# A retention, convolution and expert kernel on one core: the quarter tiles' pieces placed one or two hooks later, and their expert index read once

## The chip, the cores and the metric

The kernel runs on one core of one Trainium2 chip. The metric is the device time of an execution in microseconds (us). Times shown as "before" are the median of three executions and the range of the three; the profile is of one more execution, taken by the hardware profiler.

## The reference

Three layers follow one another. Only the last one is touched by the change:

```python
def _moe2_ref(x, w_gate, w_local, w1, w2):
    B, S, D = x.shape                      # 2, 768, 512; 8 experts, F = 1024
    logits = einsum('bsd,de->bse', x, w_gate)
    local_gate = sigmoid(x @ w_local)
    for b in range(B):
        prev_e = -1
        for s in range(S):
            fresh_e = argmax(logits[b, s])
            e = fresh_e if s == 0 or local_gate[b, s] < 0.5 else prev_e
            prev_e = e
            p = softmax(logits[b, s])
            h = maximum(x[b, s] @ w1[e], 0.0)
            out[b, s] = p[e] * (h @ w2[e])
```

Here x is the output of a retention layer (state and outer products over 768 steps, 8 heads) followed by a gated feed-forward layer with a convolution of three taps. Every token goes to exactly one expert, which is found only at run time.

## The kernel before, in words

The first 230 us compute the retention layer, the feed-forward layer and the routing. What the change touches is the expert stage, the function `experts` (line 958), which runs for the rest of the time.

The tokens are sorted by expert into **tiles** of 128 tokens (eleven are handled by this stage, j = 0 to 10) and into **quarters** of 32 tokens for what an expert has left over. Four quarters, each with an expert of its own, make one **group**; there are two, g = 0 and 1. A tile's matmuls run in three passes over weights split into a high and a low part (`mm3`, lines 134 to 136). A group's matmuls run once, in plain 32-bit floats, and need the weights of four experts.

*Weights of a tile.* `fetch(j, which)` (line 699) issues four transfers of 512 KB from SP's queue, for the first matrix (which = 0) or the second. From tile 1 on it first reads the expert's index from the table `ei` into a register (`expert_at`, line 691), and from tile 2 on also a flag that says whether this tile's expert differs from that of tile j - 2, whose weights sit in the same buffer. If it doesn't, the four transfers are issued and move nothing. `cut(j, which, i)` (line 725) splits half of a fetched matrix on ACT and DVE, and `g1`, `g2` multiply with the halves.

*Weights of a group.* `fetch_q(g, which, i)` (line 713) fetches the i-th quarter of the first or second matrix of four experts: four transfers of 512 KB (line 723), each preceded by a read of that expert's index (line 692). We call such four transfers a **piece**: a0 to a3 are the pieces of group 0's first matrices, b0 to b3 those of its second, and A0 to A3, B0 to B3 those of group 1. Two buffers take turns for the pieces: `qc` (even ones) and `qs1l` (odd ones). A new piece can be fetched only when the matmuls of the piece two before it are done, which is why `fetch_q` of the next pieces is called from within the group's own code (`follow`). Pieces a0 and a1 are fetched ahead.

*The order of the work.* Every engine runs its instructions in the order in which the code writes them. The tiles' code calls `hook()` (line 951) after each half of `g1` and of `g2`: twice ahead of the loop, then four times per tile, so that hook 4j+3 follows the first half of g1 of tile j+1, 4j+4 its second half, 4j+5 the first half of g2 of tile j and 4j+6 its second half. The groups are generators (`group`, line 894) with seven steps: 1 turn the 32 x 4 token rows (line 818), 2 the matmuls with the first two pieces (line 916), 3 those with the next two, 4 the relu, 5 turn the hidden rows, 6 and 7 the matmuls with the b pieces, two each (line 938). The list `QT` (line 947) names the hooks at which the next step is written. A step that calls `follow` writes the next `fetch_q` at that place of SP's queue too.

```python
QT = [3, 8, 8, 9, 13, 18] + [19, 22, 26, 26, 27, 31, 36]
```

Step 1 of group 0 isn't in the list: it stands in the loop's code, right after the first half of g1 of tile 1.

Of the kernel before, what the change touches and what calls it, by code (L numbers as in the profile page):

```python
# [29 lines left out]
NTILE = 16  # L30
# [62 lines left out]
def tile_kernel(ctx, tc, cat, cst, qT, kT, kN, vN, w_in, conv_w, w_out, wg, w1, w2, out):  # L93
# [346 lines left out]
    for i in range(len(seq) + LOOK):  # L440
        if i < len(seq):
            p, c = seq[i]
# [12 lines left out]
        if i >= LOOK:  # L455
            p, c = seq[i - LOOK]
# [226 lines left out]
    SLOT = ["s0h", "s0l", "s1h", "c5"]  # L683
    QSLOT = ["c4", "s1l"]
    ncut, nq = [0], [0]
    W, QW = {}, {}

    def home(tag):
        return big if tag[0] == "s" else ws if tag == "c4" else wx

    def expert_at(n):
        return sy.value_load(ei[0:1, 0, n:n + 1], min_val=0, max_val=E - 1)  # L692
# [6 lines left out]
    def fetch(j, which, parts=range(4)):  # L699

        src = (w1, w2)[which].rearrange("e p a n -> e p (a n)")
        kw = {}
        if j == 0:
            src = src[0]
        else:
            src = src[bass.ds(expert_at(j), 1)].rearrange("o p n -> (o p) n")
            if j > 1:
                kw = dict(cond=sy.value_load(ei[0:1, 1, j:j + 1], min_val=0, max_val=1), cond_hint=True)
        dst = raw(j % 2, which)
        for i in parts:  # L710
            sy.dma_start(out=dst[:, i, :], in_=src[:, i * 1024:(i + 1) * 1024], **kw)

    def fetch_q(g, which, i, parts=range(4)):

        if (g, which, i) not in QW:
            tag = QSLOT[nq[0] % 2]
            nq[0] += 1
            QW[g, which, i] = home(tag).tile([P, 4, 1024], F32, tag=tag, name="q" + tag)
        w = QW[g, which, i]
        src = (w1, w2)[which].rearrange("e p a n -> e p (a n)")  # L720
        for u in parts:
            one_e = src[bass.ds(expert_at(NTILE + 4 * g + u), 1)].rearrange("o p n -> (o p) n")
            sy.dma_start(out=w[:, u, :], in_=one_e[:, i * 1024:(i + 1) * 1024])  # L723

    def cut(j, which, i):

        tag = SLOT[ncut[0] % len(SLOT)]
        ncut[0] += 1
        w = home(tag).tile([P, 2, 2, 1024], F32R, tag=tag, name="w" + tag)
        for h in range(2):  # L730
            r = RAW[j % 2, which][:, 2 * i + h, :]
            se.activation(out=w[:, 0, h, :], in_=r, func=AF.Copy)  # L732
            ve.tensor_tensor(out=w[:, 1, h, :], in0=r, in1=w[:, 0, h, :].bitcast(F32), op=ALU.subtract)  # L733
        W[j, which, i] = w.rearrange("p s h n -> p s (h n)")
# [3 lines left out]
    def gather(j, n=NT):  # L738

        X[j] = xg = xpool[0].tile([P, DM], F32, name="xg")  # L740
        po.memset(xg, 0.0)
        return po.indirect_dma_start(out=xg, out_offset=None, in_=xs[0:n], in_offset=bass.IndirectOffsetOnAxis(ap=it[:, j:j + 1], axis=0),  # L742
                                     bounds_check=n - 1, oob_is_err=False)
# [45 lines left out]
    for n, (t, m) in enumerate(units, 1):  # L789
        ffn_out(1, t, (m,))  # L790
        for step in STEPS.get(n, ()):
            next(step, done)
        if n in (20, 28):
            cut(0, 0, n // 28)
        if n == 27:
            for j in range(2):
                gather(j, NT - 2 * P)
        if n == 32:
            fetch(1, 0)
        if n == 40:  # L800
            fetch_q(0, 0, 0)
# [26 lines left out]
    def begin_x(j):  # L828

        x, X[j] = X[j], psb.tile([P, 4, P], F32, tag="b", name="tp")  # L830
        for k in range(4):
            te.matmul(X[j][:, k, :], x[:, k * P:(k + 1) * P], ident, start=(k == 0), stop=False, skip_group_check=True)
        late_x(j, 0)
# [6 lines left out]
    def turn_x(j):  # L840

        if j < 2:
            late_x(j, 1)
        hi, lo = (wk.tile([P, 4, P], F32R, name="x" + n) for n in "hl")
        x = X.pop(j)
        ps = x if j < 2 else turn(x, 0)
        split(ps, hi, lo)
        XT[j] = hi, lo

    def turn_h(j):  # L850

        t = [wk.tile([P, 8, P], F32R, name="t" + n) for n in "hl"]
        hr = HR.pop(j)
        ps = [turn(hr, i) for i in (0, 4)]
        for i in (0, 4):
            split(ps[i // 4], t[0][:, i:i + 4, :], t[1][:, i:i + 4, :])
        return t

    def g1(j, i, h):
        xh, xl = XT[j]  # L860
        w = W.pop((j, 0, i))
        for n in range(2):
            for k in (2 * i, 2 * i + 1):
                o = slice((k % 2) * F + n * 512, (k % 2) * F + (n + 1) * 512)
                mm3(h[n], xh[:, k, :], xl[:, k, :], w[:, 0, o], w[:, 1, o], k == 0, k == 3)

    def relu(j, h):
        HR[j] = hr = wk.tile([P, F], F32, name="hr")
        for n in range(2):
            se.activation(out=hr[:, n * 512:(n + 1) * 512], in_=h[n], func=AF.Relu)  # L870

    def g2(j, i, t, y):
        hh, hl = t
        w = W.pop((j, 1, i))
        for k in range(4 * i, 4 * i + 4):
            o = slice((k % 4) * DM, (k % 4 + 1) * DM)
            mm3(y, hh[:, k, :], hl[:, k, :], w[:, 0, o], w[:, 1, o], k == 0, k == 7)

    def finish(j, last=False):
        if last:  # L880
            yo = wk.tile([P, F], F32, tag="hr", name="yo")[:, 0:DM]
        elif j >= NTILE:
            yo = wk.tile([P, F], F32, tag="hq", name="yo", bufs=1)[:, 0:DM]
        else:
            yo = wk.tile([P, DM], F32, name="yo", bufs=1)
        se.activation(out=yo, in_=Y.pop(j), func=AF.Copy, scale=pr[:, j:j + 1])  # L886
        po.indirect_dma_start(out=rows_of[j], out_offset=bass.IndirectOffsetOnAxis(ap=it[:, j:j + 1], axis=0),  # L887
                              in_=yo, in_offset=None, bounds_check=NT - 1, oob_is_err=False)

    def tile_g1():  # L890
        return [psa.tile([P, 512], F32, tag=f"a{n}", name="g1") for n in range(2)]


    def group(g, ahead=None):
# [6 lines left out]
        def follow():  # L901
            p = pieces.pop(0)
            if p and p not in QW:
                fetch_q(*p)
# [39 lines left out]
                yield  # L944


    QT = [3, 8, 8, 9, 13, 18] + [19, 22, 26, 26, 27, 31, 36]
    groups = []
    hooks = [0]

    def hook():
        hooks[0] += 1
        while QT and QT[0] <= hooks[0]:
            QT.pop(0)
            while groups and next(groups[0], done) is done:
                groups.pop(0)

    def experts(n):

        fetch_q(0, 0, 1)  # L960
        fetch(1, 1)
        for j in range(2):
            begin_x(j)
        for j in range(2):
            turn_x(j)
        gather(NTILE)
        gather(2)
        groups.extend(group(g, g + 1 < QSTAT) for g in range(QSTAT))
        h = tile_g1()
        for i in range(2):  # L970
            g1(0, i, h)
            cut(1, 0, i)
            if i:
                relu(0, h)
            hook()
        cut(0, 1, 0)
        fetch(2, 0)
        T = {}
        for j in range(n):
            last, ahead = j + 1 == n, j + 2 < n  # L980
            if j + 3 < n:
                fetch(j + 3, 0)
            if j > 0:
                finish(j - 1)
            if j + 3 < n:
                gather(j + 3)
            if j == 2:
                gather(NTILE + 1)
            if j not in T and j > 0:
                T[j] = turn_h(j)  # L990
            if not last:
                h = tile_g1()
                g1(j + 1, 0, h)
                if j == 0:
                    next(groups[0])
                    T[j] = turn_h(j)
                    cut(0, 1, 1)
                if ahead:
                    cut(j + 2, 0, 0)
                hook()  # L1000
                g1(j + 1, 1, h)
                if ahead:
                    cut(j + 2, 0, 1)
                relu(j + 1, h)
                hook()
            if ahead:
                turn_x(j + 2)
                fetch(j + 2, 1)
            Y[j] = y = psb.tile([P, 512], F32, tag="b", name="y")
            for i in range(2):  # L1010
                g2(j, i, T[j], y)
                if not last:
                    cut(j + 1, 1, i)
                    if not ahead and i == 0:
                        T[j + 1] = turn_h(j + 1)
                    hook()
        finish(n - 1, True)
        assert not QT

# [68 lines left out]
```

## Time and profile before

| | |
|---|---|
| median of three executions (range) | 429.79 us (428.33 to 430.05) |
| the profiled execution | 426.66 us |
| its span, first to last instruction | 424.9 us |
| PE busy, DVE, ACT, POOL | 96%, 68%, 60%, 22% of the span |
| mean granted TensorE clock | 0.997 of full speed |
| bytes moved by the transfers | 86.59 MB, mean 204 GB/s over the span |

How to read it: the busy share of PE counts a matmul as busy from its start to a modelled end, so a PE that waits between two matmuls can look busy. Waits are read better from the starts of neighbouring matmuls. The mean of 204 GB/s is an average over stages with little traffic (the first half) and stages with much (the expert stage).

### The profile page before, as it was taken

Reading aid. Unit: us, or ns where it says so; the run is one execution under the profiler, and the core shown is the slowest. Engines: PE = TensorE matmul, PEld = TensorE weight load, DVE = VectorE, ACT = ScalarE, POOL = GpSimd, SP = SyncE. Lnnn points to the kernel's source line nnn. Section 1 sums busy time; section 2 is a strip of 40 time slices with the busy share of each in tenths; the row PEclk is TensorE's granted clock in tenths of the full one; section 3 lists DMA queues with packets and bytes.
Section 4 is the critical chain, followed back from the end, with each engine's and each line's share of the span. In section 5 each row is a group of like instructions: output and inputs, shape, how many; then the busy total and the mean of one; then the engine's idle time right before and its main releaser. Section 6 shows DMA issues by size and latency. Waiting matters only on the chain.

```text
span 424.9 us, 7234 instructions
## 1 busy us (share of the span) xinstructions
PE 409.8 (96%) x2412; PEld 329.4 (78%) x2412; DVE 290.4 (68%) x494; ACT 256.8 (60%) x405; POOL 92.6 (22%) x92
## 2 busy tenths in 40 slices
PE   8999999999999999999999999899999999999992
PEld 7898999998887888988788848476848566776881
DVE  3799989798873712677994576748675684859650
ACT  2786678577762233667232576658667585958660
POOL 5356756231100000000003310305303202111210
PEclk9999999999999999999999999999999999999998
DMA  7989762320000110000575999999969999766001
GB/s 245 382 311 391 276 234 63 111 78 2 0 2 0 76 49 25 2 0 2 200 271 159 376 405 367 386 359 411 375 280 333 401 367 324 321 213 257 20 25 54
DMA packets 27324, 86.59 MB, mean 204 GB/s; under 512 B 3598, under 2 KB 4622, under 8 KB 27280
## 3 DMA queue, kind: packets, MB, share of 16 engines
q1 hardware_dynamic: 25200, 79.76, 51.1%
q0 software_dynamic: 2080, 6.29, 3.9%
q8 instruction: 21, 0.34, 0.3%
q14 instruction: 23, 0.19, 0.1%
HBM read 105.18 MB, written 6.55 MB: 263 GB/s over the span
## 4 chain that ended last, share of the span: by engine, by line
PE 53%; issue 21%; DMA 10%; SPq 5%; POOL 4%; DVE 4%; ACT 2%; POOLq 0%
PE h_ps L134 6%; PE x_ps L134 6%; PE h_ps L135 5%; PE h_ps L136 5%; PE x_ps L136 5%; PE x_ps L135 5%; DMA qs1l<-in_w_dram 4%; PE y L304 3%; PE s_ps L284 3%; DMA r<-in_w_dram 3%; POOL out_dram L887 3%; SPq L692 2%; DMA qc<-in_w_dram 2%; PE y L306 2%; SPq L723 2%
## 5 line engine op out<-in xcount | busy, mean ns | idle before, releaser
L134 PE MATMUL h_ps<-xT,wih 128*128 128x384 f32 x128 | 46.6, 364 | 0.1
L887 POOL DMA_INDIRECT out_dram<-yo,it x13 | 16.4, 1259 | 137.8 <-ACT yo L886 137.5
L366 DVE SCALAR_TENSOR_TENSOR cc<-h,cw,cc 128x768 f32<-128x768 f32 x32 | 34.8, 1088 | 15.9 <-ACT cc L363 15.8
L742 POOL DMA_INDIRECT xg<-xs,it x13 | 18.4, 1417 | 122.5 <-DVE pr L678 108.4
L135 PE MATMUL h_ps<-xT,wih 128*128 128x384 f32 x128 | 43.1, 337 | 0.0
L136 PE MATMUL h_ps<-xT,wil 128*128 128x384 f32 x128 | 43.1, 336 | 0.0
L134 PE MATMUL x_ps<-woh,hg 128*128 128x512 f32 x96 | 38.5, 401 | 0.0
L136 PE MATMUL x_ps<-woh,hg 128*128 128x512 f32 x96 | 37.5, 391 | 0.0
L135 PE MATMUL x_ps<-wol,hg 128*128 128x512 f32 x96 | 37.5, 390 | 0.0
L155 POOL TENSOR_TENSOR na<-na,raw 128x512 int32<-128x512 int32 (+1 forms) x17 | 23.0, 1354 | 50.7 <-DVE na L153 25.7
L733 DVE TENSOR_TENSOR wc<-r,wc 128x1024 fp32r<-128x1024 f32 x22 | 26.0, 1221 | 10.7 <-ACT wc L732 10.6
L733 DVE TENSOR_TENSOR ws1h<-r,ws1h 128x1024 fp32r<-128x1024 f32 x22 | 26.0, 1221 | 9.5 <-ACT ws1h L732 9.1
L733 DVE TENSOR_TENSOR ws0h<-r,ws0h 128x1024 fp32r<-128x1024 f32 x22 | 26.1, 1222 | 8.3 <-ACT ws0h L732 8.3
L732 ACT ACTIVATE wc<-r 128x1024 fp32r<-128x1024 f32 x22 | 22.1, 1053 | 13.8 <-PE g L136 13.8
L304 PE MATMUL y<-at,vz 128*128 128x128 f32 x192 | 29.5, 275 | 0.6 <-ACT vz L279 0.6
L284 PE MATMUL s_ps<-qz,kq 128*128 128x256 f32 x96 | 29.1, 385 | 1.0 <-DVE qz L253 1.0
L733 DVE TENSOR_TENSOR ws0l<-r,ws0l 128x1024 fp32r<-128x1024 f32 x22 | 26.0, 1221 | 5.6 <-ACT ws0l L732 5.5
L732 ACT ACTIVATE ws0l<-r 128x1024 fp32r<-128x1024 f32 x22 | 22.1, 1053 | 8.6 <-PE y L136 8.6
L304 PEld LDWEIGHTS y<-at,vz 128*128 128x128 f32 x192 | 25.9, 192 | 1.2 <-ACT vz L279 0.8
L134 PEld LDWEIGHTS h_ps<-xT,wih 128*128 128x128 f32 x128 | 24.1, 189 | 3.3 <-issue 1.8
L286 DVE TENSOR_TENSOR at<-s_ps,ca 128x256 f32<-128x256 f32 x48 | 20.1, 420 | 7.5 <-PE s_ps L284 6.9
L732 ACT ACTIVATE ws1h<-r 128x1024 fp32r<-128x1024 f32 x22 | 22.1, 1053 | 5.2 <-PE g L136 4.8
(234 smaller groups left out, 1028.8 us busy)
## 6 DMA issues: line engine op xcount, KB each, us to landing
r<-in_w_dram SPq DMA_DIRECT2D x88, 512.0 KB
qc<-in_w_dram SPq DMA_DIRECT2D x32, 512.0 KB
qs1l<-in_w_dram SPq DMA_DIRECT2D x32, 512.0 KB
raw<-in_w_in_dram SPq DMA_DIRECT2D x8, 512.0 KB
raw<-in_w_out_dram SPq DMA_DIRECT2D x8, 512.0 KB
kq<-in_qT_dram SPq DMA_DIRECT2D x7, 384.0 KB
kq<-in_kT_dram SPq DMA_DIRECT2D x7, 384.0 KB
kv<-in_vN_dram SPq DMA_DIRECT2D x7, 384.0 KB
```

Of the source, the lines that this page charges most:

```text
L134: te.matmul(ps, lhi, rhi, start=first, stop=False)
L135: te.matmul(ps, lhi, rlo, start=False, stop=False)
L136: te.matmul(ps, llo, rhi, start=False, stop=last)
L155: po.tensor_tensor(out=a, in0=a, in1=lo, op=ALU.add)
L284: te.matmul(ps, self.kq[:, 0, tok], self.qz[:, :, tok], start=True, stop=True)
L286: ve.tensor_tensor(out=self.at[c], in0=ps, in1=self.dm, op=ALU.mult)
L304: te.matmul(y, vz[:, c, j, :], at[:, j, :], start=(j == 0), stop=(c == 0 and j == 1))
L366: ve.scalar_tensor_tensor(out=cc, in0=h[:, i:i + S], scalar=cw[:, m, i:i + 1], in1=cc, op0=ALU.mult, op1=ALU.add)
L732: se.activation(out=w[:, 0, h, :], in_=r, func=AF.Copy)
L733: ve.tensor_tensor(out=w[:, 1, h, :], in0=r, in1=w[:, 0, h, :].bitcast(F32), op=ALU.subtract)
L742: return po.indirect_dma_start(out=xg, out_offset=None, in_=xs[0:n], in_offset=bass.IndirectOffsetOnAxis(ap=it[:, j:j + 1], axis=0), bound ...
L887: po.indirect_dma_start(out=rows_of[j], out_offset=bass.IndirectOffsetOnAxis(ap=it[:, j:j + 1], axis=0), in_=yo, in_offset=None, bounds_ch ...
```

## The change

Two edits. The first moves steps of the groups to other hooks: step 1 of group 0 from the loop's code (between hooks 2 and 3) to hook 4, its steps 2 to 7 from hooks 3, 8, 8, 9, 13, 18 to hooks 5, 10, 10, 11, 15, 19, and the seven steps of group 1 from hooks 19, 22, 26, 26, 27, 31, 36 to hooks 20, 24, 28, 28, 29, 33, 38. The second reads the index of a quarter's expert once, at the first piece that needs it, and keeps it in a register for the seven other pieces.

```diff
-    W, QW = {}, {}
+    W, QW, QE = {}, {}, {}
...
         for u in parts:
-            one_e = src[bass.ds(expert_at(NTILE + 4 * g + u), 1)].rearrange("o p n -> (o p) n")
+            if (g, u) not in QE:
+                QE[g, u] = expert_at(NTILE + 4 * g + u)
+            one_e = src[bass.ds(QE[g, u], 1)].rearrange("o p n -> (o p) n")
...
-    QT = [3, 8, 8, 9, 13, 18] + [19, 22, 26, 26, 27, 31, 36]
+    QT = [4, 5, 10, 10, 11, 15, 19] + [20, 24, 28, 28, 29, 33, 38]
...
                 if j == 0:
-                    next(groups[0])
                     T[j] = turn_h(j)
```

**SP's queue, where pieces a2 and a3 are issued.** `r10` and `r00` are the buffers of the first matrix of odd and even tiles, `r11` and `r01` those of the second; `qc4` and `qs1l` are the buffers of the pieces; `ei` is the table of indices. Before:

```order
L711 DMA r10_2037<-in_w1_dram 128x1024
L692 TENSOR_LOAD ei_1427
L692 ISA x2
L723 ISA
L723 DMA qc4_2690<-in_w1_dram 128x1024
...
L723 DMA qs1l_2739<-in_w1_dram 128x1024
L692 TENSOR_LOAD ei_1427
L692 ISA x2
L708 TENSOR_LOAD ei_1427
L708 ISA x2
L711 ISA
L711 DMA r01_2032<-in_w2_dram 128x1024
```

Now:

```order
L711 DMA r01_2032<-in_w2_dram 128x1024
L725 ISA
L725 DMA qc4_2723<-in_w1_dram 128x1024
...
L725 DMA qs1l_2736<-in_w1_dram 128x1024
L692 TENSOR_LOAD ei_1427
L692 ISA x2
L708 TENSOR_LOAD ei_1427
L708 ISA x2
L711 ISA
L711 DMA r00_2027<-in_w1_dram 128x1024
```

The fetch of tile 2's second matrix (r01) now stands ahead of the two pieces instead of behind them, and the pieces' eight transfers have no reads between them.

Over the whole stage the order of SP's fetches, four transfers to each name, goes as follows (t3.1 is the first matrix of tile 3, t3.2 its second):

```
before: a0 a1 | t1.2 t2.1 t3.1 | a2 a3 | t2.2 t4.1 | b0 b1 | t3.2 t5.1 t4.2 | b2 b3 | t6.1 t5.2 | A0 A1 | t7.1 t6.2 | A2 A3 | t8.1 t7.2 | B0 B1 | t9.1 t8.2 t10.1 | B2 B3 | t9.2 t10.2
now:    a0 a1 | t1.2 t2.1 t3.1 t2.2 | a2 a3 | t4.1 t3.2 | b0 b1 | t5.1 t4.2 t6.1 | b2 b3 | t5.2 t7.1 | A0 A1 | t6.2 t8.1 | A2 A3 | t7.2 t9.1 | B0 B1 | t8.2 t10.1 t9.2 | B2 B3 | t10.2
```

**PE, where the matmuls with pieces b2 and b3 stand.** `yq_ps` is the group's output, `y` that of a tile's g2, `g` that of g1, `hr` and `xg` the rows to be turned. Before:

```order
L136 MATMUL y<-ws0l,tl 128x512
L938 MATMUL yq_ps<-qc_3283,tq 32x512 x8
L938 MATMUL yq_ps<-qs1l,tq 32x512 x8
L818 MATMUL tp<-cs,hr 128x128 x8
L134 MATMUL g_3694<-ws1h,xh 128x512
...
L136 MATMUL g_3695<-ws1h,xl 128x512
L818 MATMUL tp<-cs,xg 128x128 x4
```

Now:

```order
L136 MATMUL y<-ws0l,tl 128x512
L820 MATMUL tp<-cs,hr 128x128 x8
L134 MATMUL g_3339<-ws1h,xh 128x512
...
L136 MATMUL g_3340<-ws1h,xl 128x512
L940 MATMUL yq_ps<-qc_3187,tq 32x512 x8
L940 MATMUL yq_ps<-qs1l,tq 32x512 x8
L134 MATMUL g_3339<-wc_3217,xh 128x512
```

The turn of tile 4's hidden rows and the first half of g1 of tile 5 now stand ahead of the two pieces' matmuls. At the group's other steps the same move is of two hooks.

## Rows read from the trace of the kernel before

**Rows 1.** Windows view: us, PE, PEld, DVE, ACT, POOL busy; clock, DMA share, GB/s.

```profile
240.00:250.00 10.00, 9.38 (x52) 7.19 (x54) 7.39 (x8) 7.67 (x12) 5.13 (x5) 1.00 1.03 408
275.84:316.83 40.99, 40.82 (x221) 28.14 (x221) 28.77 (x28) 28.02 (x36) 9.87 (x8) 1.00 0.97 372
282.00:284.00 2.00, 2.00 (x10) 1.61 (x9) 1.78 (x2) 1.62 (x3) 0.00 (x0) 1.00 0.93 309
316.00:318.00 2.00, 1.83 (x11) 0.38 (x10) 0.54 (x1) 0.00 (x0) 0.00 (x0) 1.00 0.02 6
```

**Rows 2.** PE's timeline, group 0's first matrices: start, us, what, idle before.

```profile
247.80 0.66 PE L818 MATMUL tp<-cs,xg 128*128 128x128 f32 x4 [0.62 <-DMA xg<-xs,it]
249.26 1.92 PE L916 MATMUL hq_ps<-qc,xq 128*32 128x512 f32 x16
254.70 0.50 PE L134 MATMUL g<-wc,xh 128*128 128x512 f32 x1
...
269.93 1.92 PE L916 MATMUL hq_ps<-qc,xq 128*32 128x512 f32 x16
275.84 1.90 PE L916 MATMUL hq_ps<-qs1l,xq 128*32 128x512 f32 x10 [1.05 <-DMA qs1l<-in_w_dram]
277.67 0.55 PE L818 MATMUL tp<-cs,xg 128*128 128x128 f32 x3
```

**Rows 3.** PE's timeline, group 0's second matrices.

```profile
294.21 1.92 PE L938 MATMUL yq_ps<-qc,tq 128*32 128x512 f32 x16
297.79 0.50 PE L134 MATMUL y<-ws0l,th 128*128 128x512 f32 x1
304.26 0.39 PE L134 MATMUL g<-wc,xh 128*128 128x512 f32 x1
...
312.98 1.93 PE L938 MATMUL yq_ps<-qc,tq 128*32 128x512 f32 x16
316.83 1.90 PE L938 MATMUL yq_ps<-qs1l,tq 128*32 128x512 f32 x10 [0.17 <-DMA qs1l<-in_w_dram]
318.66 1.09 PE L818 MATMUL tp<-cs,hr 128*128 128x128 f32 x8
322.36 0.60 PE L818 MATMUL tp<-cs,xg 128*128 128x128 f32 x4
```

**Rows 4.** PE's timeline, group 1's first matrices.

```profile
331.55 1.92 PE L916 MATMUL hq_ps<-qc,xq 128*32 128x512 f32 x16
335.80 0.44 PE L818 MATMUL tp<-cs,hr 128*128 128x128 f32 x2
342.20 0.60 PE L818 MATMUL tp<-cs,xg 128*128 128x128 f32 x4
348.19 1.07 PE L916 MATMUL hq_ps<-qc,xq 128*32 128x512 f32 x8
353.40 0.77 PE L818 MATMUL tp<-cs,hr 128*128 128x128 f32 x5
```

**Rows 5.** Chain of waits, two links between SP's issues: start, us, what.

```profile
238.47 7.50 DMA qc<-in_w_dram
245.99 11.90 DMA r<-in_w_dram
```

**Rows 6.** SP's timeline, issues of transfers: start, us to the last one's end, what.

```profile
229.89 1.95 SPq L711 DMA_DIRECT2D r<-in_w_dram  x4
252.95 0.08 SPq L711 DMA_DIRECT2D r<-in_w_dram  x1
258.01 0.33 SPq L711 DMA_DIRECT2D r<-in_w_dram  x1
259.19 3.71 SPq L723 DMA_DIRECT2D qc<-in_w_dram  x4
316.90 0.07 SPq L711 DMA_DIRECT2D r<-in_w_dram  x1
317.82 3.70 SPq L723 DMA_DIRECT2D qc<-in_w_dram  x4
```

## The prediction

> **What bounds the kernel now.** I read the page's busy shares first (PE 96%), then the windows and PE's timeline of the expert stage, because a matmul's end is modelled and a waiting PE can look busy. Read by the starts of neighbouring matmuls, PE's timeline has no gap in the expert stage except at the groups' steps. A pair of pieces that waits for nothing takes 297.79 - 294.21 = 3.58 us [rows 3]. The other five pairs of the stage's first half take longer: a0 and a1 254.70 - 249.26 = 5.44, a2 and a3 277.67 - 269.93 = 7.74 [rows 2], b2 and b3 318.66 - 312.98 = 5.68 [rows 3], A0 and A1 335.80 - 331.55 = 4.25, A2 and A3 353.40 - 348.19 = 5.21 [rows 4]. Less 3.58 each that is 1.86 + 4.16 + 2.10 + 0.67 + 1.63 = 10.42 us, and 0.62 us more go at 247.80, where step 1 waits for its gathered rows [rows 2]. **11.04 us** is all that better placing can give. B0 to B3 wait for nothing.
>
> The wait ends each time with the last transfer of the odd piece, at 275.84 and 316.83 for instance [rows 2, 3]; 1.83 us later the pair is done (277.67, 318.66), so a pair loses nothing if its last transfer lands within 3.58 - 1.83 = 1.75 us of its start.
>
> Why do they land late? The windows show the transfers at a DMA share of 1.03 early in the stage and 0.97 from 275.84 to 316.83 us, at 408 and 372 GB/s [rows 1]: there the transfers, not their issue, set the pace. The chain of waits shows what paces SP: the issue at 245.99 is the eighth after that at 238.47 and was released by the latter's landing, and the one at 258.01 is again the eighth after 245.99 [rows 5, 6]. So at most eight transfers are under way. Fetches that move nothing take places too: their issues last 0.07 to 0.08 us against 0.33 [rows 6]. Read one by one, those of tiles 2, 5, 6, 8, 9 and 10 are such (12 fetches, 48 issues); tiles 3, 4 and 7 really fetch.
>
> **The change part by part.**
>
> *The reads.* 56 reads of an index go (64 before, 8 after). A piece's four issues span 3.71 us, so (3.71 - 0.33)/3 = 1.13 us lie between two; tile 1's first fetch, which reads nothing in between, has (1.95 - 0.33)/3 = 0.54 [rows 6]. That is about 0.6 us of SP's queue each, 33 us in all. On the path I take it as zero: up to 317 us SP waits for the places of earlier transfers, and 1.13 us is less than the 1.46 us that a transfer takes there (below). Its bound on the gain side is a faster stretch of transfers, priced as a rival.
>
> *The moved transfers up to b3.* Ahead of b3's last transfer stand the same real ones in both orders: a0, a1, t1.2, t3.1, a2, a3, t4.1, b0, b1, t3.2, t4.2, b2, b3. Only their order differs (t3.2 moves ahead of b0 and b1; the empty t2.2 ahead of a2). From a3's last landing to b3's, 275.84 to 316.83, 28 of 512 KB pass in 40.99 us, 1.464 each, gathers and scatters included [rows 1 to 3]. As long as no gap opens, b3 lands at 316.8 us again. **This sets the gain up to there, not the 8.7 us that stand in the pairs before it.** I looked for gaps. a2 now stands behind the empty t2.2, whose two reads and four short issues put it, as an estimate, 2 us behind the 259.19 of before [rows 6]; t3.1 is still being moved until 257.89 + 4 x 1.464 = 263.7 [rows 5]. b2 stands behind t4.2, whose last transfer gets its place when b1 lands (299.3, below), and behind the empty t6.1, so at about 302.5; t4.2 is moving until 275.84 + 20 x 1.464 = 305.1. Neither is late, by little.
>
> *PE up to b3.* With b3 landing at 316.83, its pair again ends at 318.66, but PE has by then done one hook's work more (the turn of tile 4's rows and half a g1), which before ran from 318.66 to 322.36 [rows 3]: **3.70 us gained**. That PE gets there in time: step 1 moves behind half a g1, and its rows, landing at 247.80, are there. Tile 2's rows, turned right behind, were gathered after those; if they are late, that costs under 1 us, which the next waits take up. a0 and a1 no longer wait. PE comes to a2 at 269.93 - 0.62 - 1.86 = 267.45 plus a turn and two halves of g2; a turn and two halves take 304.26 - 297.79 = 6.47 us [rows 3], so at 273.9. a3 lands at 275.84, allowed until 275.7: some 0.2 us lost instead of 4.16, and the pair ends at 277.67 as before. From there to b0 lay 16.54 us, 294.21 - 277.67 [rows 2, 3]; now the 6.47 us done earlier leave it and as much comes in with hook 15 in place of 13, so b0 starts at 294.2 again. b1's last is now the 16th after a3, landing at 275.84 + 16 x 1.464 = 299.3, behind t3.2: **a new wait** of 299.3 - 1.75 - 294.2 = 3.3 us; the pair ends at 301.1. From there to b2 lie 312.98 - 304.26 + 3.70 = 12.4 us, so PE is at b2 at 313.5 and loses 1.6 us until b3. Waits of 0.2, 3.3 and 1.6 us remain of 8.74.
>
> *Group 1.* Before, hardly anything moved between 316 and 318 us (6 GB/s) [rows 1], since the fetch behind b3 was of two empty ones and A0 was issued only at 317.82 [rows 6]. Now t7.1 is issued there and A0 behind it: A1's last is the 12th after b3, landing at 316.83 + 12 x 1.464 = 334.4. PE starts A0 at 318.66 + (342.20 - 322.36) - 4.25 = 334.25 [rows 3, 4] and allows 336.0: no wait, **0.67 us gained**. A2 and A3 can be issued when the pieces A0 and A1 are used up, 336.0 and 337.8; eight transfers of 1.464 land 11.7 us behind that, between 347.7 and 351.0 (from the later point, with one transfer's time on top to begin). PE does a tile's work before it gets there, 348.19 - 335.80 = 12.4 us [rows 4], is at A2 at 350.2 and allows 352.0: no wait, **1.63 us gained**. Bounds for these two: nothing, and 2.30 together. B0 to B3 had no wait and have over 10 us of room.
>
> *The rest.* ACT and DVE run the same operations; steps 4 and 5 keep their place behind step 3. The tail is the same.
>
> **The sum.** 3.70 + 0.67 + 1.63 = 6.0 us. The profiled execution took 426.66 us with a span of 424.9; it would take 420.7. The median of the three runs is 429.79, 3.1 above it, and I take the gain from that: **423.8 us**.
>
> **The rivals.**
>
> *Faster transfers, more gained.* If the reads did thin out the stream, the stretch runs at its best, 408 GB/s instead of 372 [rows 1]: 40.99 x 372/408 = 37.4 us, b3 lands 3.6 us sooner. PE without any wait would end b3 at 318.66 - 8.74 + 3.70 = 313.6, so it can use the 3.6 us: 420.2. For it: the lowest window, 309 GB/s at 282, lies where pieces were issued 1.13 us apart [rows 1, 6]. Against: with eight under way the issue isn't what is waited for. The Trainium skill ("DMA: Bandwidth & Descriptors", Specifications) speaks against it too: it gives some 358 GB/s as what HBM leaves one core, and by that limit the stretch would take 40.99 x 372/358 = 42.6 us and 1.6 us of the gain would go. The trace disagrees: 408 GB/s over 10 us [rows 1].
>
> *Group 1 stays as late as it was.* t7.1 waits for its buffer, or A2 and A3 begin too late behind A0 and A1: only 3.7 us are gained, 426.1. For it: A3 has only 1 to 4 us of room.
>
> *Nothing measurable.* b3 lands 2 us later through gaps at a2 and b2, and group 1 keeps its waits: 1.7 us gained, 428.1.
>
> *Slower: the eight places run half empty.* Behind a2 stand four empty places, around t4.2 eight; with only two to four real transfers under way the stream thins. The price is the lowest window, 309 GB/s: the 28 would take 40.99 x 372/309 = 49.3 us, b3 lands 8.3 us later, and 8.3 - 6.0 = 2.3 us are lost: 432.1. It decides against the change when the stretch falls below 372 x 40.99/(40.99 + 6.0) = 325 GB/s on average. Against: empty places stood in the old order too, and the stretch still made 372.
>
> **How the numbers follow.** The forecast (gain of 4.8 to 7.2 us) has a chance of 0.45, faster transfers 0.2, group 1 as late as before 0.2, nothing 0.1, slower 0.05. About 0.5%, 2.15 us, is what a measurement of this kernel can tell from no change: faster 0.85, same 0.10, slower 0.05. The range leaves out half of the last two cases and the far end of the second: 420.0 to 428.0, its likeliest part 422.6 to 425.0.
>
> **What would show it.** In the new profile: no wait for step 1's rows and for a1; a wait at a3 under 1 us, at b1 of about 3.3 and at b3 of about 1.6 us; b3's last landing within 1.5 us of 316.8; no empty window behind it; A0 to A3 at 3.6 us a pair; the span at 419. It is wrong if b3 lands outside 314 to 319, or if PE waits at a tile's own matmuls (lines 134 to 136), where it doesn't now.

## The result, and the profile after

| | before | after |
|---|---|---|
| median of six executions each, on one chip (range) | 428.57 us (427.13 to 430.05) | 423.72 us (422.8 to 425.39) |
| ratio after to before, 95% interval | | 0.989 (0.9857 to 0.9923) |
| the profiled execution, its span | 426.66 us, 424.9 us | 423.19 us, 421.4 us |
| first matmul of the expert stage to the end ("the stage" below) | 424.9 - 233.13 = 191.77 us | 421.4 - 233.42 = 187.98 us |

The change gains 4.85 us by the medians, 3.3 to 6.1 us by the interval. The stage is the better measure for a profile: what runs ahead of it is the same in all kernels here, yet its first matmul starts anywhere from 233.1 to 235.5 us, ahead of all the steps that were moved. One profile is one execution, though: a second profile of the changed kernel (the last experiments below) has a stage of 187.36 us, 0.6 us shorter, so a difference of that size between two profiles tells nothing.

PE's timeline after the change, at the steps of both groups (start, us, what, idle before and its releaser):

```profile
256.22 1.92 PE L918 MATMUL hq_ps<-qc,xq 128*32 128x512 f32 x16 [1.52 <-ACT xq L910]
259.80 0.50 PE L134 MATMUL y<-ws0l,th 128*128 128x512 f32 x1
...
274.98 1.92 PE L918 MATMUL hq_ps<-qc,xq 128*32 128x512 f32 x16
278.59 0.66 PE L820 MATMUL tp<-cs,hr 128*128 128x128 f32 x4
...
295.53 1.92 PE L940 MATMUL yq_ps<-qc,tq 128*32 128x512 f32 x16
300.43 1.90 PE L940 MATMUL yq_ps<-qs1l,tq 128*32 128x512 f32 x10 [0.42 <-DMA qs1l<-in_w_dram]
302.26 0.50 PE L134 MATMUL g<-wc,xh 128*128 128x512 f32 x1
...
314.75 1.92 PE L940 MATMUL yq_ps<-qc,tq 128*32 128x512 f32 x16
318.90 1.90 PE L940 MATMUL yq_ps<-qs1l,tq 128*32 128x512 f32 x10 [0.21 <-DMA qs1l<-in_w_dram]
320.73 0.50 PE L134 MATMUL g<-wc,xh 128*128 128x512 f32 x1
...
336.36 1.93 PE L918 MATMUL hq_ps<-qc,xq 128*32 128x512 f32 x16
339.93 0.66 PE L820 MATMUL tp<-cs,xg 128*128 128x128 f32 x4
...
352.36 1.93 PE L918 MATMUL hq_ps<-qc,xq 128*32 128x512 f32 x16
355.93 0.66 PE L820 MATMUL tp<-cs,xg 128*128 128x128 f32 x4
```

Read it like [rows 2 to 4]: a pair that waits for nothing takes 3.57 to 3.61 us. So a0/a1 (259.80 - 256.22) and a2/a3 no longer wait, nor do A0/A1 and A2/A3. b1 now waits 302.26 - 295.53 - 3.58 = 3.15 us, a wait that before did not exist, and b3 waits 320.73 - 314.75 - 3.58 = 2.40 us. The wait for step 1's gathered rows [rows 2] is gone; a wait of 1.52 us for the copy `xq` on ACT is new. Together 1.52 + 3.15 + 2.40 = 7.1 us of waits instead of 11.04, and 3.79 us less in the stage.

The chain of waits of the same kernel, its longest links from 245 to 319 us (start, us, what):

```profile
245.84 11.91 DMA r<-in_w_dram
...
257.87 5.64 DMA r<-in_w_dram
...
266.06 10.65 DMA qs1l<-in_w_dram
...
276.82 12.62 DMA r<-in_w_dram
...
289.46 10.93 DMA qs1l<-in_w_dram
...
300.50 5.99 DMA r<-in_w_dram
...
308.67 10.19 DMA qs1l<-in_w_dram
```

The seven links add up to 67.9 of the 73 us from 245.84 to 318.86, all of them transfers: the end of this stretch is b3's landing at 308.67 + 10.19 = 318.86. The windows of the same kernel (us; busy time of PE, PEld, DVE, ACT, POOL; clock; DMA share; GB/s) show where the stream of transfers is thin:

```profile
262.00:264.00 2.00, 2.00 (x15) 1.74 (x14) 0.06 (x1) 1.15 (x2) 0.00 (x0) 1.00 0.84 246
275.84:318.90 43.06, 42.09 (x230) 27.06 (x223) 29.42 (x30) 28.22 (x38) 11.96 (x11) 1.00 1.01 382
298.00:306.00 8.00, 7.36 (x33) 3.64 (x31) 1.09 (x1) 0.69 (x1) 0.86 (x1) 1.00 0.95 334
316.00:318.00 2.00, 1.88 (x13) 0.39 (x6) 2.00 (x2) 0.86 (x1) 1.73 (x2) 1.00 1.01 309
```

Where [rows 1] has 6 GB/s at 316 us there are now 309: t7.1 is under way. But up to b3's landing there are two thin places, at 262 us where a2 is issued and from 298 to 306 us where b2 is.

### The profile page after: what moved, and what is told of

It is laid out like the page before. It is cut to its first block, busy times and chain, and to the rows that moved or that the text cites. A ratio compares the mean times of both kernels' runs of the same rounds, so it can differ in the third digit from the quotient of the medians.

```text
span 421.4 us, 7062 instructions
## 1 busy us (share of the span) xinstructions
PE 406.2 (96%) x2412; PEld 329.0 (78%) x2412; DVE 290.0 (69%) x494; ACT 256.7 (61%) x405; POOL 93.4 (22%) x92
## 3 DMA queue, kind: packets, MB, share of 16 engines
q1 hardware_dynamic: 25200, 79.76, 51.3%
## 4 chain that ended last, share of the span: by engine, by line
PE 65%; DMA 20%; issue 5%; DVE 4%; SPq 2%; ACT 1%; POOL 1%; POOLq 0%
DMA r<-in_w_dram 9%; DMA qs1l<-in_w_dram 8%; PE h_ps L134 6%; PE x_ps L134 6%; PE h_ps L135 5%; PE h_ps L136 5%; PE x_ps L136 5%; PE x_ps L135 5%; PE y L304 3%; PE s_ps L284 3%; PE y L134 2%; PE y L136 2%; PE y L135 2%; PE yq_ps L940 2%; PE g L134 2%
## 5 line engine op out<-in xcount | busy, mean ns | idle before, releaser
L502 ACT ACTIVATE xn<-x_ps 128x512 f32<-128x512 f32 x10 | 6.0, 598 | 31.4 <-PE x_ps L136 13.8
```

## The experiments

Piece and fetch names are those used above. In each kernel the stage is measured from its first matmul to the end. "Wait" of a pair is its length less 3.58 us.

**The two edits, each alone.** The reads alone (kernel before, index kept in a register) and the places alone (kernel before, new hooks):

```diff
-    QT = [3, 8, 8, 9, 13, 18] + [19, 22, 26, 26, 27, 31, 36]
+    QT = [4, 5, 10, 10, 11, 15, 19] + [20, 24, 28, 28, 29, 33, 38]
...
-                    next(groups[0])
```

> The kernel before with the index of a quarter's expert read once, and every step of the groups at its old hook. Theory (the transfers up to b3 set the pace, not their issue): the pairs of pieces end where they ended before, a2 and a3 near 277.7 us, b2 and b3 near 318.7 us; span 424 to 425.5 us, less than 1 us from the 424.9 us of before. Rival (the 56 reads are what thins out the stream): b3 lands 2 to 4 us sooner, the wait at b3 of 2.1 us goes, span 421 to 423 us, most of the change's gain.

> The new hooks, with the index read ahead of every transfer as before. Theory: most of the gain stays; a2 and b2 are issued 1 to 3 us later behind the empty fetches, because four reads of 0.6 us stand among their issues, so the stream has a longer gap there and b3 lands 0 to 2 us behind the 318.9 us of the changed kernel; span 421.5 to 423.5 us against 421.4. Rival (the reads are the gain): span back at 424 to 425.

The reads alone: 426.98 us, ratio 0.9981 (0.9952 to 1.0011), stage 191.95 against 191.77: no difference that can be measured. Why they are free in the old order stands in SP's waits, for which line was waited and for how long in all (us, times, longest). First the kernel before, then that with the reads taken out:

```profile
SPq L711 <- DMA qs1l<-in_w_dram: 11.6, 14, 1.7
...
SPq L711 <- DMA r<-in_w_dram: 4.7, 6, 1.4
SPq L711 <- DMA qc<-in_w_dram: 2.4, 3, 1.3
...
SPq L723 <- DMA r<-in_w_dram: 1.0, 2, 0.6
```

```profile
SPq L711 <- DMA qs1l<-in_w_dram: 23.2, 26, 2.1
SPq L711 <- DMA qc<-in_w_dram: 14.1, 16, 2.9
SPq L725 <- DMA r<-in_w_dram: 7.6, 11, 1.0
SPq L711 <- DMA r<-in_w_dram: 4.0, 5, 1.5
```

By these lines SP waited 19.7 us for the landing of earlier transfers; without the reads it waits 48.9 us. So 29 of the 33 us of reads that the prediction estimated came back as waiting.

The places alone: 426.43 us, ratio 0.9945 (0.992 to 0.9969). Its profiled execution took 423.48 us, with a stage of 188.02 us, just as after; but that was the lowest of its twelve executions, and the median gains only half of what the whole change gains. In the profiled execution the pairs wait 7.1 us in all (1.52 at a0, 0.93 at a3, 1.84 at b1, 2.74 at b3, 0.11 at A1), as after. With the reads, the stream at a2 is thinner still, in the window view 88 GB/s where after has 246:

```profile
262.00:264.00 2.00, 2.00 (x15) 1.74 (x14) 0.00 (x0) 0.97 (x2) 0.00 (x0) 1.00 0.36 88
```

By the medians the reads may cost something in the new order (0.9945 against 0.989, some 2.4 us), perhaps where SP has to refill a thin stream; the profiles show no such cost, and SP's waits for landings, 41.7 us in the after kernel and 14.9 us in this one, say that most of the reads come back as waiting here too. The two kernels weren't measured side by side on one chip, and this stays open.

**Each group's move alone.** After, with group 1's old hooks; and after, with group 0's old hooks and its step 1 back in the loop:

```diff
-    QT = [4, 5, 10, 10, 11, 15, 19] + [20, 24, 28, 28, 29, 33, 38]
+    QT = [4, 5, 10, 10, 11, 15, 19] + [19, 22, 26, 26, 27, 31, 36]
```

```diff
-    QT = [4, 5, 10, 10, 11, 15, 19] + [20, 24, 28, 28, 29, 33, 38]
+    QT = [3, 8, 8, 9, 13, 18] + [20, 24, 28, 28, 29, 33, 38]
...
+                    next(groups[0])
```

> Reads once and group 0 at the new hooks, group 1 at its old ones (19, 22, 26, 26, 27, 31, 36). Theory: up to b3 as in the changed kernel, b3's pair ends near 320.7 us with one hook's work more done; but tile 7's first matrix now stands ahead of A0 and A1, A1 lands at about 336.5 us, and PE comes to A0 at about 330: a wait of about 4.8 us at A1 where it had 0.67, none at A3; nearly all is given back, span 425 to 426.5 us. Rival (each group's move is worth its own waits): span about 422 to 423.

> Reads once and group 1 at the new hooks, group 0 at its old ones. Theory: up to b3 as before, pair ending near 318.7 us; A0 to A3 no longer wait, 0.67 + 1.63 = 2.3 us gained; span 422 to 423.5 us. Rival (group 1's waits come from the stream's backlog, which only group 0's move takes away): A1 and A3 wait as before, span 424.5 to 425.5.

Group 0 alone: 427.81 us, ratio 1.0003 (0.998 to 1.0026), stage 192.62, 0.85 us longer than before. PE's timeline of this kernel at A0 and A1 shows where the time went:

```profile
332.02 2.63 PE L918 MATMUL hq_ps<-qc,xq 128*32 128x512 f32 x15
...
338.27 1.90 PE L918 MATMUL hq_ps<-qs1l,xq 128*32 128x512 f32 x10 [0.21 <-DMA qs1l<-in_w_dram]
340.11 1.09 PE L820 MATMUL tp<-cs,hr 128*128 128x128 f32 x8
```

The pair takes 8.09 us, a wait of 4.5. Counted from the stage's first matmul (at 235.28), PE comes to A0 1.7 us sooner than before, and A1's last transfer lands 2.2 us later, because t7.1's four transfers now stand ahead of A0 and A1, as was expected. Group 1 alone: 424.75 us, ratio 0.9899 (0.9871 to 0.9928), stage 189.08, 2.7 us shorter than before, of which 2.3 us lie behind b3's pair; A0 to A3 wait for nothing. By these profiles group 0's move is worth 189.08 - 187.98 = 1.1 us on top of group 1's, and nothing without it; the ratios, 0.9899 and 0.989, don't tell the two kernels apart.

**What sets b3's landing: bytes or places?** After, without the fetch of t3.2 (four real transfers ahead of b0 and b1); and after, with t4.2 (ahead of b2) under tile 2's flag, so that it is issued and moves nothing:

```diff
-                fetch(j + 2, 1)
+                if j != 1:
+                    fetch(j + 2, 1)
```

```diff
-                kw = dict(cond=sy.value_load(ei[0:1, 1, j:j + 1], min_val=0, max_val=1), cond_hint=True)
+                flag = 2 if (j, which) == (4, 1) else j
+                kw = dict(cond=sy.value_load(ei[0:1, 1, flag:flag + 1], min_val=0, max_val=1), cond_hint=True)
```

> The changed kernel without the fetch of tile 3's second matrix (four transfers that stood ahead of b0; tile 3 then multiplies with what its buffer holds, tile 1's matrix, so the output of that expert's tiles isn't the reference's). Theory (28 transfers behind a3 set b3's landing): 24 stand there now, b1 and b3 land about 6 us sooner, the waits at b1 (3.15 us) and b3 (2.40 us) go: span 415.5 to 416.5 us against 421.4. Rival (these waits are set by issue or by PE's own order): span within 1 us of 421.4.

> The changed kernel with tile 4's second matrix fetched under tile 2's flag, which is off: the four issues stay in SP's queue and take their places but move nothing (tile 4 then multiplies with the matrix that its buffer holds, so the output of that expert's tiles isn't the reference's). Theory (bytes, not places): b1 waits as before, 3.15 us; b3 lands 5 to 6 us sooner and its wait of 2.40 us goes: span 418.5 to 419.5 us against 421.4. Rival (the eight places, half of them empty, pace the stream): b3 waits as before, span 421 to 422.

Without t3.2: 419.22 us, ratio 0.9761 (0.9697 to 0.9825), stage 183.22. The waits at b1 and b3 are gone, as the starts of b0, b2 and what follows them show (298.61 + 1.83 = 300.44 ends the first pair):

```profile
296.87 1.92 PE L940 MATMUL yq_ps<-qc,tq 128*32 128x512 f32 x16
298.61 1.90 PE L940 MATMUL yq_ps<-qs1l,tq 128*32 128x512 f32 x16
...
312.94 1.92 PE L940 MATMUL yq_ps<-qc,tq 128*32 128x512 f32 x16
314.68 1.90 PE L940 MATMUL yq_ps<-qs1l,tq 128*32 128x512 f32 x16
```

So PE does end this stretch by the transfers ahead of b1 and b3. The stage is 4.76 us shorter than after's, where 4.9 to 5.9 were expected; a3 waited 1.0 us in this run.

With t4.2 empty: 423.71 us, ratio 0.9874 (0.9806 to 0.9941), stage 187.18. Counted from the stage's first matmul, b3's pair ends at 86.22 us, in the after kernel at 87.31, and b3 still waits 1.4 us. With four real transfers fewer ahead of it, b3 landed some 1 us sooner and not the 5 to 6 us that were expected: the theory that bytes alone decide **fell**. The windows of this kernel say why:

```profile
300.00:302.00 2.00, 1.79 (x12) 0.38 (x10) 0.71 (x1) 0.00 (x0) 0.48 (x1) 1.00 0.39 118
302.00:304.00 2.00, 2.00 (x8) 1.24 (x7) 0.00 (x0) 0.00 (x0) 0.00 (x0) 1.00 0.08 31
304.00:306.00 2.00, 2.00 (x12) 1.68 (x11) 0.00 (x0) 0.40 (x1) 0.00 (x0) 1.00 0.42 102
```

The stream nearly stops. Twelve empty issues (t5.1, t4.2, t6.1) stand ahead of b2. Those of t5.1 and t4.2 take the places of b0's and b1's transfers and wait for their landings, and so all the real transfers ahead must land before b2 can be issued. (t6.1's four find empty issues eight places before them and wait for nothing.) The theory from here on: **an empty fetch costs its place among the eight**.

**Moving the empty fetches behind the pieces.** After, with t2.2 written behind a2 and a3 and t6.1 behind b2 and b3:

```diff
-            if j + 3 < n:
+            if j + 3 < n and j != 3:
                 fetch(j + 3, 0)
...
+                if j == 3:
+                    fetch(6, 0)
...
-                fetch(j + 2, 1)
+                if j > 0:
+                    fetch(j + 2, 1)
...
+                    if j == 0 and i == 0:
+                        fetch(2, 1)
```

> The changed kernel with two empty fetches moved: that of tile 2's second matrix behind a2 and a3, that of tile 6's first behind b2 and b3. Theory (gaps where a2 and b2 stand behind empty fetches put b3's landing at 318.9 in place of 316.8 us): a2 is issued 2 us sooner and b2 3 us sooner, the thin windows at 262 (246 GB/s) and 298 to 306 us (334 GB/s) fill, b3 lands 1 to 2.3 us sooner: span 419 to 420.5 us against 421.4. Rival (the empty fetches thin the stream wherever they stand): span within 0.5 us of 421.4.

426.8 us, ratio 0.9946 (0.9917 to 0.9975), stage 190.81: b3's pair ends 2.45 us sooner after the stage's start than in the after kernel, and then all of it is lost at A0 and A1, whose pair takes 8.92 us (a wait of 5.3). Eight empty issues, t6.1 and t5.2, now stand between b3 and t7.1, and in the windows of this kernel the stream stops there:

```profile
318.00:320.00 2.00, 2.00 (x16) 0.38 (x10) 1.50 (x2) 0.05 (x1) 1.27 (x1) 1.00 0.02 8
```

The same thing as in the kernel before at 316 us [rows 1]: behind eight empty issues in a row the stream is empty.

**Everything from b2 on one hook later.**

```diff
-    QT = [4, 5, 10, 10, 11, 15, 19] + [20, 24, 28, 28, 29, 33, 38]
+    QT = [4, 5, 10, 10, 11, 16, 20] + [21, 25, 29, 29, 30, 34, 39]
```

> The changed kernel with b0 and b1 at hook 16, b2 and b3 at hook 20 and all of group 1 one hook later. Theory (b3's landing is set by the transfers, so each hook's work ahead of it is gained as long as PE is early): half a g1, 2.86 us, moves ahead of b3, the waits at b1 and b3 fall from 5.55 to about 2.7 us, group 1 still waits for nothing: span 418 to 419 us against 421.4. Rival (the pieces' fetches follow the hooks and b3 lands later with them): span within 0.5 us of 421.4.

426.73 us, ratio 0.9961 (0.9929 to 0.9992), stage 191.28. b1 waits for nothing, and PE does half a g1 more before b3's pair ends, as expected; but A2 and A3 now stand behind t7.2 on SP's queue, which I had overlooked, and their pair waits 4.4 us (PE's timeline of this kernel):

```profile
352.68 2.17 PE L918 MATMUL hq_ps<-qc,xq 128*32 128x512 f32 x16
...
358.87 1.90 PE L918 MATMUL hq_ps<-qs1l,xq 128*32 128x512 f32 x10 [0.44 <-DMA qs1l<-in_w_dram]
360.70 0.50 PE L134 MATMUL y<-ws0l,th 128*128 128x512 f32 x1
```

PE also waits 1.27 us for the copy `tq` on ACT (line 930), a wait that the changed kernel doesn't have.

**The last four, on one chip with the kernel before.** The changed kernel again; the one-hook-later kernel with t7.2 moved behind A2 and A3; the changed kernel with no empty fetches; and both of the latter together:

```diff
-                fetch(j + 2, 1)
+                if j != 5:
+                    fetch(j + 2, 1)
...
                     hook()
+                    if j == 5 and i == 0:
+                        fetch(7, 1)
```

```diff
     def fetch(j, which, parts=range(4)):
+        if j in (2, 5, 6, 8, 9, 10):
+            return raw(j % 2, which)
```

> The changed kernel once more, on the same chip as the three that follow, so that they can be set beside it. Expected: span 421.4, stage 188.0 us from its first matmul to the end, ratio to before 0.989; waits of 3.15 us at b1 and 2.40 us at b3.

> All of group 0's steps from b2 on and all of group 1's one hook later, as in the run before this one, and the fetch of t7.2 moved behind the step that uses A2 and A3. Theory (the steps' places decide, through what stands ahead of each piece): b1 waits for nothing, b3 under 2.2 us, A0 to B3 for nothing; the stage is 4.4 us shorter than with t7.2 ahead of A2 and A3 (191.3), at 186.9, or 185.5 if the wait for tq goes too: span 418.9 to 420.3 against 421.4. Rival (t7.2 is only late in another place): its four transfers, some 6 us later than before, hold up tile 7's cuts and so PE at tile 7's second matrix; the stage is at 188 or above.

> The changed kernel without the fetches of tiles 2, 5, 6, 8, 9 and 10, which move nothing with these inputs; the output is the same with them. Theory (an empty fetch costs its place among the eight, and eight in a row let the stream run dry): no thin stretch at 262 and at 298 to 306 us, b3 lands at about 316.8 in place of 318.9, the waits at b1 and b3 fall from 5.55 us together to about 3.5, and the stage is 2 us shorter, at 186.0; as an upper end, with every transfer at 408 GB/s as in the best window, b3 lands before PE asks for it and the stage is at 182.5. Rival (only the bytes ahead of b3 decide): b3 lands within 0.5 us of 318.9, stage 188.0.

> The two kernels before this one together: places one hook later, t7.2 behind A2 and A3, no empty fetches. Theory: the places give PE work to do until b3 lands, the missing empties let b3 land sooner, so both count: stage 184 to 185. Rival (one of the two makes the other worthless): as the better of the two alone.

| | median us (range), six each | ratio to before | stage us |
|---|---|---|---|
| changed kernel again | 422.78 (422.11 to 425.89) | 0.9875 (0.9828 to 0.9921) | 187.36 |
| one later, t7.2 behind | 422.15 (421.11 to 423.28) | 0.9846 (0.9803 to 0.9889) | 187.26 |
| no empty fetches | 419.73 (417.48 to 422.93) | 0.9793 (0.9742 to 0.9844) | 183.46 |
| both | 418.65 (418.29 to 420.31) | 0.9763 (0.9722 to 0.9803) | 183.42 |

The changed kernel again: a0, a3, b1 and b3 wait 1.52, 1.2, 2.0 and 2.1 us (their pairs take 259.52 - 255.95, 279.55 - 274.75, 302.05 - 296.50 and 320.24 - 314.54), where 1.52, 0, 3.15 and 2.40 were seen before. The sum, 6.8 us, agrees with the first profile's 7.1; how it falls on a3 and b1 differs by over 1 us between two executions of one kernel, and the expectation of 3.15 us at b1 missed.

One later with t7.2 behind: the wait at A2 and A3 is gone, and PE waits at no matmul of tile 7, so the rival (t7.2 late in another place) found nothing, but the stage missed the forecast of 185.5 to 186.9 by a little. What the later places save at b1 came back as other waits: 1.87 us at b3, 1.27 us for the copy `tq`, and 0.84 us for gathered rows. It can't be told apart from the changed kernel.

No empty fetches: the theory held; the stage, 183.46 us, lies between its 186.0 and its upper end of 182.5. The windows of this kernel, from b1 to the landing of b3 and at the two places that were thin:

```profile
262.00:264.00 2.00, 2.00 (x13) 1.63 (x12) 0.00 (x0) 0.14 (x1) 0.00 (x0) 1.00 1.03 397
276.73:315.50 38.77, 38.77 (x231) 26.67 (x223) 28.28 (x29) 28.35 (x38) 10.90 (x11) 1.00 1.03 408
298.00:306.00 8.00, 8.00 (x47) 5.01 (x39) 3.21 (x3) 2.86 (x4) 1.70 (x1) 1.00 1.02 408
```

The stream runs at 408 GB/s throughout. SP's timeline shows the cause at b2 (start, us to the last one's end, what). First the changed kernel, then that without empty fetches:

```profile
291.35 12.38 SPq L711 DMA_DIRECT2D r<-in_w_dram  x12
303.98 2.86 SPq L725 DMA_DIRECT2D qc<-in_w_dram  x4
```

```profile
291.24 2.92 SPq L713 DMA_DIRECT2D r<-in_w_dram  x3
298.50 1.97 SPq L727 DMA_DIRECT2D qc<-in_w_dram  x4
```

Twelve issues, eight of them empty, hold SP for 12.4 us, and b2 is issued at 303.98. Without the empty ones it is issued at 298.50, 5.5 us sooner (6.5 counted from the stage's first matmul), as soon as its buffer is free (b0's matmuls end at 298.26).

An empty fetch costs SP in two ways, and this run takes out both. In the changed kernel t5.1's four empty issues wait for b0's landings (SP's waits from 289.8 to 295.4 us: us, times, longest); t6.1's four wait for nothing, and still the index and the flag read ahead of them and the issues themselves (SP's timeline) fill the 3.15 us from t4.2's last issue to b2's first:

```profile
SPq L711 <- DMA qc<-in_w_dram: 2.7, 3, 0.9
```

```profile
302.37 1.36 SPq L711 DMA_DIRECT2D r<-in_w_dram  x4
```

For the places speaks the chain of waits shown above: its links at 257.87 and 300.50, and the issues at 263.53 and 306.51 with which a2 and b2 go on, each wait for the landing of the issue eight places before, with four empty ones in between. What the places and SP's own time are worth apart wasn't measured. PE's timeline of the kernel without empty fetches, at b2 and b3:

```profile
313.21 1.92 PE L942 MATMUL yq_ps<-qc,tq 128*32 128x512 f32 x16
314.95 2.45 PE L942 MATMUL yq_ps<-qs1l,tq 128*32 128x512 f32 x16
317.33 0.50 PE L134 MATMUL g<-wc,xh 128*128 128x512 f32 x1
```

The pair takes 4.12 us, a wait of 0.54 instead of 2.40 (2.1 in the repeat), and b1 waits 0.60 instead of 3.15 (2.0). Both changes together can't be told from this one, as the rival had it. But the later places did cover what was left: b1 and b3 no longer wait there at all. What that saves, 1.14 us, went into the wait of 1.27 us for the copy `tq`, which comes with the later places.

The version without empty fetches beats both kernels, but holds only for inputs in which those six tiles share the expert of the tile two before; that is known only at run time. A kernel that skips them by a branch on SP's queue wasn't tried, so what the branch would cost is open.

## Why the prediction was right, and where it was off

The time was forecast as 423.8 us and came out as 423.72; the direction and the mechanism (waits for the last transfer of odd pieces) are as told. The closeness is partly luck: the forecast took a gain of 6.0 us off a median of three executions, 429.79; the six executions of the comparison have 428.57, and the gain is 4.85 us. An overestimate of 1.2 us was taken from a start that was 1.2 us high. By the medians alone 6.0 isn't refuted (3.3 to 6.1 us by the interval; 6.0 in the repeat, 428.78 - 422.78). The profiles show that it was too much: the stage gained 3.79 us, 4.41 in the repeat, and the span, foretold as 419 us, was 421.4.

- *The reads, zero.* Right for the old order, by the 29 us that turned from reads into waits. In the new order the medians leave room for some 2.4 us, not settled. The rival "faster transfers", which rested on the reads thinning out the stream, was right that 408 GB/s can be had, and about right that it would be worth 3.6 us: without empty fetches the median is 3.05 us and the stage 3.9 us below the changed kernel's on the same chip. It named the wrong cause.
- *b3 lands at 316.8 again: the step that failed.* It landed at 318.86, 0.14 us inside the 319 beyond which the prediction would have called itself wrong. This was the term "3.70 us gained up to b3": relative to the stage's start and to the work done, b3's pair ends 320.73 - 233.42 = 87.31 us after it, against 318.66 - 233.13 + 3.70 = 89.23 with the old landing, so 1.9 us were gained; in the repeat 320.24 - 233.14 = 87.10, so 2.1. The prediction asked whether a2 and b2 would be issued before the last transfer ahead of them had landed, and answered "neither is late, by little". By that test neither was: a2 was issued at 261.35 (estimated 2 us behind 259.19) and t3.1 landed at 257.87 + 5.64 = 263.51; b2 was issued at 303.98 (estimated 302.5) and t4.2 landed at 300.50 + 5.99 = 306.49. It is the test that failed: a last transfer still under way doesn't keep the stream full while most of the eight places are empty. At a2 it fell to 246 GB/s, around b2 to 334, and without the empty fetches both places run at about 400. b1's last transfer landed at 300.4, not 299.3; from b1's landing to b3's, 12 transfers took 18.46 us, 1.54 each in place of 1.464. The 1.464 itself was an average over a stretch with empty places in it; without them the same 12 took 315.50 - 298.87 = 16.63 us, 1.39 each (landings read as the pair's end less 1.83 us).
- *The waits.* Forecast: a3 0.2, b1 3.3, b3 1.6 us; measured: 0, 3.15 and 2.40, in the repeat 1.2, 2.0 and 2.1. In the first profile b1's came out right because two errors cancel: PE came to b0 1.3 us later than forecast, and the landing was 1.1 us late.
- *The copy `xq`.* Not foreseen: 1.52 us at a0. ACT makes the copy at 255.56 us only, behind cuts and a relu that keep it busy from 247.94 on, while the turn that it copies was issued at 250.92; before, the copy was made at 248.50, right behind the turn. In the changed kernel PE waits for b1 and b3 later on in any case. In the two kernels without empty fetches, where those waits are small or gone, this one is still 1.34 and 1.52 us; what its removal would bring wasn't tried.
- *Group 1, 2.30 us.* Right: A0 to A3 wait for nothing, and the stage's whole gain of 3.79 us (4.41 in the repeat) less the 1.9 (2.1) up to b3 leaves 1.9 (2.3).
- *The rival "nothing measurable"* held in its first half: it had b3 land 2 us later through gaps at a2 and b2, with 1.7 us gained up to there, which is what happened. Its second half, group 1 keeping its waits, did not. 1.7 + 2.30 = 4.0 us is nearer to what the stage gained than the forecast's 6.0.
- *The signs.* As foretold, step 1's rows and a1 are not waited for, A0 to A3 take 3.6 us a pair, and PE waits at no tile's own matmuls: its idle times over 0.15 us in the stage all lie at the groups' steps.
- *The slower rival* (eight places half empty) had the mechanism that cost the missing part, with a price far too high: the stretch ran at 382 GB/s, not at 309 (which wasn't even the lowest window of before: from 314 to 316 us it had 272). The two kernels that put twelve or eight empty issues in a row show it at its worst, 31 to 118 GB/s over 6 us in the one and 8 GB/s over 2 us in the other.

One rule was weighed in the prediction, the 358 GB/s that the Trainium skill ("DMA: Bandwidth & Descriptors", Specifications) gives for one core. The Trainium skill ("HBM Reference", Specifications (TRN2)) also says that a core streaming alone measures about 425 GB/s, bounded by its DMA engines, and that the share is what is left when both cores of a pair stream. The run without empty fetches agrees with the second: 408 GB/s over 38.77 us, at a DMA share of 1.03.

## What to carry to other kernels

Where a program keeps a fixed number of transfers under way, count its issues in places, not in bytes: here an issue that moves nothing waits, like any other, until the transfer eight places ahead has landed, and eight in a row let the stream run dry. An issue that waits for nothing still takes its queue's time. A step that is moved to meet its data must be followed to the next step and the next fetch behind it on the queue; group 0's move gained nothing without group 1's, and one hook more put two pieces behind a fetch that nobody had been waiting for. An average rate of transfers read from a trace has its gaps built in; look for the best window, and for what makes the others worse. A wait read from one profile is one execution's: a3 and b1 differed by over 1 us between two profiles of one kernel, and only their sum and the stage's length held.

## What the runs showed of the hardware that was not expected

- A conditional transfer that moves nothing is not free, although its issue takes 0.07 to 0.08 us of SP [rows 6]: without the 48 of them, and the reads of index and flag that go with them, the median fell from 422.78 to 419.73 us, and the page of either kernel lists the same 79.76 MB on the queue of these transfers.
- The eight places are the program's: on SP's queue eight semaphores take turns, and each issue waits for the landing that the issue eight before it reports on the same one. How many transfers the hardware would take without that wait, no run here shows.
- Without empty issues among the eight places the stream holds 408 GB/s for 38.77 us beside a busy PE; the 372 GB/s of [rows 1] was not the most that the transfers can do but the mean of full and half-empty stretches.
- The DMA share doesn't tell a full stream from a thin one: a share of 1.01 stands beside 309 GB/s from 316 to 318 us in the changed kernel, 1.02 beside 408 from 298 to 306 us without empty fetches. The prediction took a share of 0.97, with 372 GB/s beside it, for transfers that set the pace.
